# One written order for all five engines from attention into the experts, and the last batch's routing moved in among the early tiles

## The chip, the cores and the metric

The kernel runs on one core of a Trainium2 chip. That core has TensorE (PE in the profile; its weight loads stand apart as PEld), VectorE (DVE), ScalarE (ACT), GpSimd (POOL) and SyncE (SP). Each engine works through its own queue of instructions in that queue's order, and engines wait for each other through semaphores. The metric is the device time of one execution in microseconds (us), the median of several runs. The profile is one further execution, and its span is the time from the first to the last instruction of the core.

## What is computed

Two blocks follow each other. The first is an attention in which a query sees only the keys of its own hash bucket (six sign bits of a random projection). The second sends each token to one of eight experts.

```python
B, H, S, D = 4, 8, 768, 64
mask   = bucket(q)[:, :, :, None] == bucket(k)[:, :, None, :]
scores = where(mask, q @ k.T / sqrt(D), -1e9)
attn   = exp(scores - max);  attn = attn / (sum(attn) + 1e-9)
x      = (attn @ v) as (B*S, H*D)                       # 3072 tokens, 512 wide
logits = (x/|x|) @ (emb/|emb|).T / tau                  # 8 experts
e      = argmax(logits);  gate = softmax(logits)[e]
out    = gate * (relu(x @ w1[e]) @ w2[e])               # w1: 512 x 1024, w2: 1024 x 512
```

## The kernel before

**Attention.** The 32 heads are taken as 16 pairs (`pairs`, four pairs for each of four batches). A pair has 12 units: two halves of the queries by six chunks of 128 keys. For one unit `scores` does the matmuls (L541, L544), an exponential on ACT (L547) and a running sum over the chunks on DVE (L551, L554); `attend` multiplies by the values (L566). The main loop (L676) takes three units at a time, g = 0 to 3 within a pair, and hangs one piece of side work on each g: loads and transposes for pairs to come, `sums` and `scale` for the softmax denominators of the pair before, `store` of finished rows to DRAM (`xd`), and the routing of the batch before (`logits`, `turn_logits`, `route`, `gates`, `begin`/`place`, `fill`, `lists`, `places`). The last pair has no successor to hang its denominators on; `scale_last` does them after the loop.

**Experts.** Tokens of one expert lie in tiles of 128. `fetch` gathers the rows of a tile from `xd` by four indirect DMAs on POOL (L376) into one of four buffers `xgs`, and the tile's gates by one more (L384). `turn` transposes the gathered rows on DVE (L395). `hidden` is the first layer: for each of eight blocks f, TensorE fills one of four PSUM banks `ps_h` (L906) and ACT evicts it through a relu into `ht` (L908). `result` is the second layer (L914), the weighting by the gate on DVE (L918) and a scatter to the output by an indirect DMA on POOL (L919). Each expert has `KT` = 3 planned tiles. For the experts 0 and 1 (`EARLY` = 2) the first two tiles hold tokens of the first three batches alone, so they run before the last batch is routed. Their third tiles (`late`), and all tiles of the experts 2 to 7, need the last batch's places. Tokens beyond the planned tiles come at the end in up to `NO` further tiles behind run-time conditions.

**What sets the order.** A planner orders each engine's instructions from its own estimate of costs. `in_order(begun)` (L416) overrules it: it chains all instructions of an engine since `begun` in the order in which the program is written. It is called once, at L753, at the end of attention. What is written behind that call, the expert stage, is ordered by the planner, which may also place such an instruction between two of attention's. Three `tc.issue_after` blocks (L1000, L1033, L1046/L1051) tie single pieces of routing behind one instruction.

The stretch that the change touches most is this one, between attention and expert 2:

```python
hidden(0, early[0][0], 2 * P)                                     # L989
early[1:] = [turn(got) for got in early[1:]]
lt = logits(b, ssq[b], ps_x(), sp)
result(0, early[0][1][0:1]);  l = turn_logits(...);  route(b, l, sp);  result(0, early[0][1][1:])
count(...);  place(...);  gates(...)
hidden(1, ..., range(0, 6));  fill(...);  hidden(1, ..., range(6, NF));  places(lists(...), ...)   # L1003-L1006
late = [tiles_of(e, 2) for e in range(EARLY)]
result(1, ...);  late = [turn(got) for got in late];  result(1, ...)
for e in range(EARLY):  hidden(e, late[e][0], P);  ...;  result(e, late[e][1])
```

Of the kernel before, what the change touches and what calls it, by code (L numbers as in the profile page):

```python
# [16 lines left out]
P = 128  # L17
# [9 lines left out]
def kernel(  # L27
# [341 lines left out]

    def fetch(src, pos, t, n, width=N + 1):  # L370
        parts = []
        for i in range(n):
            xg = xgs[taken[2] % len(xgs)]
            taken[2] += 1
            for g in range(NQ):
                nc.gpsimd.indirect_dma_start(  # L376
                    out=xg[:, g, :], out_offset=None, in_=xd[0 : width * NQ, :],
                    in_offset=bass.IndirectOffsetOnAxis(ap=pos[:, t + i, g : g + 1], axis=0))
            parts.append(xg)
        tiles = []  # L380
        for i in range(n):
            g = ggs[taken[1] % len(ggs)]
            taken[1] += 1
            nc.gpsimd.indirect_dma_start(out=g[:], out_offset=None, in_=gd[:, :],  # L384
                                         in_offset=bass.IndirectOffsetOnAxis(ap=src[:, t + i : t + i + 1], axis=0))
            tiles.append((i, g, src[:, t + i : t + i + 1]))
        return parts, tiles


    def turn(got):  # L390
        parts, tiles = got
        x = xgt[taken[0] % EARLY if taken[0] < 2 * EARLY else EARLY + taken[0] % NX]
        taken[0] += 1
        for i, xg in enumerate(parts):
            nc.vector.transpose(x[:, :, i * P : (i + 1) * P].rearrange("p c (g t) -> p g c t", t=32),  # L395
                                xg[:].rearrange("p g (c f) -> p g c f", f=32))
        return x, tiles

# [25 lines left out]
    with ExitStack() as at:  # L424
# [52 lines left out]
        def load(pr):  # L477
# [5 lines left out]
            for g in range(NQ):  # L483
                for i, src in enumerate((q, k)):
                    (nc.scalar if pr == 0 and i else nc.sync).dma_start(
                        qk[32 * g : 32 * (g + 1), i].rearrange("t (c a) f -> t c a f", c=NC),
                        src[b, 2 * j + g // 2].rearrange("(a t c) d -> t c a d", t=32, c=NC)[
                            :, :, :, 32 * (g % 2) : 32 * (g % 2 + 1)])
            nc.sync.dma_start(vt[:], v[b, 2 * j : 2 * j + 2].rearrange("h (p c) d -> p h c d", c=NC))
            ld[pr] = (qk, vt)  # L490


# [122 lines left out]

        def scale_last(pr):
            b, j = pairs[pr]
            z = op.tile([P, 2, SH], F32, name="zl", tag="acc", bufs=3)
            ps = banks()
            for s in range(2):  # L620
                for h in range(2):
                    nc.tensor.matmul(ps[h * D : (h + 1) * D, s, 0:SH], lhsT=ones[:, 0:D], rhs=acc[pr, s][:, h, :],
                                     start=True, stop=True)
            for s in range(2):
                nc.scalar.activation(z[:, s], ps[:, s, 0:SH], ACT.Copy, bias=TINY * S)
            t = rp.tile([P, S], F32, name="xx", tag="junk", bufs=2)
            for s in range(2):
                nc.vector.reciprocal(out=z[:, s], in_=z[:, s])
                x = xs(b)[:, j, s * SH : (s + 1) * SH]
                nc.vector.tensor_tensor(out=x, in0=x, in1=z[:, s], op=ALU.mult)  # L630
                nc.vector.tensor_tensor(out=z[:, s], in0=x, in1=x, op=ALU.mult)
            x = xs(b)[:, j - 1]
            nc.vector.tensor_tensor(out=t[:], in0=x, in1=x, op=ALU.mult)
            nc.vector.tensor_tensor(out=t[:], in0=t[:], in1=z[:].rearrange("p s n -> p (s n)"), op=ALU.add)
            nc.vector.tensor_tensor(out=ssq[b][:], in0=ssq[b][:], in1=t[:], op=ALU.add)
# [31 lines left out]
        for pr in range(3):  # L667
            load(pr)
            if pr == 0:
                nc.sync.dma_start(emb[:], expert_emb[:, :])  # L670
                nc.sync.dma_start(tau_t[:], tau.unsqueeze(0).broadcast_to([E, 1]))
        for i in range(2):
# [3 lines left out]
        for u0 in range(0, U + G, G):  # L676
# [7 lines left out]
            for u in range(u0, u0 + G):  # L684
                if u < U:
                    scores(u)
            if end and j == 2 and g == 3:
                places(listed, pos[0][:], NS, banks()[:, 0], rp)
                early = [fetch(src[0], pos[0], 0, 2, ZC + 1)]
            for u in range(u0 - G, u0):  # L690
                if 0 <= u < U:
                    attend(u)
            if pr == len(pairs):
                break
# [12 lines left out]
            elif g == 1:  # L707
                prep_features(pr + 1, 1)
                if pr > 0:
                    scale(pr - 1)  # L710
                load(pr + 3)
                if NP <= pr < NP + 2 * ND:
                    piece(pr - NP)
# [7 lines left out]
                if j == 3 and end:  # L721
                    for e in range(1, EARLY):
                        early.append(fetch(src[0], pos[0], e * KT, 2, ZC + 1))
                    bound(0)
# [13 lines left out]
            else:  # L738
# [9 lines left out]
                if j == 3 and end:  # L748
                    early[0] = turn(early[0])
        store(len(pairs) - 2)  # L750
        scale_last(len(pairs) - 1)
        store(len(pairs) - 1)
        in_order(begun)  # L753

# [122 lines left out]
    with ExitStack() as mo:  # L877
# [21 lines left out]
        ys = [mp.tile([P, DM], F32, name=f"y{i}") for i in range(3)]  # L899
        made, done, turned = [0], [None], [None]  # L900

        def hidden(i, xt, n, fs=range(NF)):
            for f in fs:
# [4 lines left out]
                nc.scalar.activation(ht[:, f, 0:n], ph[:, 0:n], ACT.Relu)  # L908

        def result(i, tiles):  # L910
            for j, gate, src in tiles:
                py = ps_y()
                for f in range(NF):
                    done[0] = nc.tensor.matmul(py[:], lhsT=ht[:, f, j * P : (j + 1) * P], rhs=w2s[i][:, f, :],  # L914
                                               start=(f == 0), stop=(f == NF - 1)).ins
                y = ys[made[0] % len(ys)]
                made[0] += 1
                turned[0] = nc.vector.tensor_scalar_mul(y[:], py[:], gate[:, 0:1]).ins  # L918
                nc.gpsimd.indirect_dma_start(out=out[:, :], out_offset=bass.IndirectOffsetOnAxis(ap=src, axis=0),  # L919
                                             in_=y[:], in_offset=None, bounds_check=N - 1, oob_is_err=False)  # L920

        def tiles_of(e, first):
            return fetch(src[1], pos[1][:], e * KT + first, KT - first)

# [63 lines left out]
        b = B - 1  # L988
        hidden(0, early[0][0], 2 * P)  # L989
        early[1:] = [turn(got) for got in early[1:]]  # L990
        lt = logits(b, ssq[b], ps_x(), sp)
        result(0, early[0][1][0:1])
        l = turn_logits(lt, ps_x(), sp)
        route(b, l, sp)
        result(0, early[0][1][1:])
        ps = ps_x()
        count(b, ps[:, 0 : E * NC], ps[:, E * NC : 2 * E * NC])
        for ins in place(b, ps[:, 0 : 2 * E * NC].rearrange("p (t n) -> p t n", t=2), sp):
            pass
        with tc.issue_after(ins.ins):  # L1000
            for i in range(3):
                gates(b, sp, i)
        hidden(1, early[1][0], 2 * P, range(0, 6))  # L1003
        fill(b, ps_x()[:, 0 : 4 * NS])
        hidden(1, early[1][0], 2 * P, range(6, NF))
        places(lists(slots, src[1][:], NS, sp), pos[1][:], NS, ps_x(), sp)  # L1006
        late = [tiles_of(e, 2) for e in range(EARLY)]
        result(1, early[1][1][0:1])
        late = [turn(got) for got in late]
        result(1, early[1][1][1:])  # L1010
        for e in range(EARLY):
            hidden(e, late[e][0], P)
            if e == 0:
                nxt = turn(tiles_of(EARLY, 0))
            bring1(e, EARLY + e)
            result(e, late[e][1])
            bring2(e, EARLY + e)
# [6 lines left out]
        for e in range(EARLY, E):  # L1024
            i = e % NW
            x, tiles = nxt
            if e + 1 < E:
                nxt = turn(tiles_of(e + 1, 0))
            else:
                nxt = turn(fetch(osrc, opos[:], 0, 1))  # L1030
            hidden(i, x, KT * P)
            if e == EARLY:
                with tc.issue_after(turned[0]):  # L1033
                    ctl, ocol = beyond_tiles()
            if e + NW < E:
# [9 lines left out]
            if e == EARLY + 1:  # L1045
                with tc.issue_after(done[0]):  # L1046
                    oslots = beyond_fill(ocol)
            elif e == EARLY + 2:
                osrc = sp.tile([P, NO], U32, name="osrc")
                opos = sp.tile([P, NO, NQ], U32, name="opos")  # L1050
                with tc.issue_after(done[0]):  # L1051
                    places(lists(oslots, osrc[:], NO, sp), opos[:], NO, ps_x(), sp)
        nt = nc.values_load(ctl[0:1, 2 * NO : 2 * NO + 1], min_val=0, max_val=NO)
        with ExitStack() as rest:  # L1054
            for t in range(NO):
# [3 lines left out]
                if t + 1 < NO:  # L1059
                    nxt = turn(fetch(osrc, opos[:], t + 1, 1))  # L1060
                hidden(i, x, P)
# [40 lines left out]
```

## Time and profile before

| what | number |
|---|---|
| time, median of 3 runs (lowest, highest) | 828.38 us (827.16, 828.94) |
| span of the profiled execution | 826.0 us |
| PE busy | 723.6 us, 88% |
| DVE / ACT / POOL busy | 357.7 / 268.2 / 221.7 us |
| mean granted TensorE clock | 0.940 |

The span falls into stages: a start without TensorE of some 10 us, attention up to about 375 us, a hand-over up to about 388 us, the experts from there. The busy share of TensorE in 40 slices is the first thing to read, since TensorE is the fullest engine; the second is the row of the clock that was granted to it. A slice is 20.65 us long. "Idle before" in a group or a timeline is the time that the engine stood still just before the instruction, followed by what ended it.

### The profile page before, as it was taken

Reading aid. Unit: us, or ns where it says so; the run is one execution under the profiler, and the core shown is the slowest. Engines: PE = TensorE matmul, PEld = TensorE weight load, DVE = VectorE, ACT = ScalarE, POOL = GpSimd, SP = SyncE. Lnnn points to the kernel's source line nnn. Section 1 sums busy time; section 2 is a strip of 40 time slices with the busy share of each in tenths; the row PEclk is TensorE's granted clock in tenths of the full one; section 3 lists DMA queues with packets and bytes.
Section 4 is the critical chain, followed back from the end, with each engine's and each line's share of the span. In section 5 each row is a group of like instructions: output and inputs, shape, how many; then the busy total and the mean of one; then the engine's idle time right before and its main releaser. Section 6 shows DMA issues by size and latency. Waiting matters only on the chain.

```text
span 826.0 us, 10015 instructions
## 1 busy us (share of the span) xinstructions
PE 723.6 (88%) x3669; PEld 360.4 (44%) x3669; DVE 357.7 (43%) x664; ACT 268.2 (32%) x432; POOL 221.7 (27%) x222
## 2 busy tenths in 40 slices
PE   4999999989998999794998113999999999999993
PEld 2444444434443444342675002654545454545481
DVE  4777887887789787855241100031100101010000
ACT  2776666656664656450110000110101010101010
POOL 4011121011211111164027772107170521010051
PEclk9999999999999999896999555999999999999997
DMA  9546546646656752223601211834343433333340
GB/s 140 91 79 97 90 85 129 118 82 115 120 106 113 123 98 39 40 56 72 206 26 42 67 48 42 302 114 164 115 165 108 153 125 128 114 128 114 128 141 20
DMA packets 198171, 87.56 MB, mean 106 GB/s; under 512 B 171473, under 2 KB 179469, under 8 KB 198104
## 3 DMA queue, kind: packets, MB, share of 16 engines
q1 hardware_dynamic: 188408, 72.94, 37.2%
q0 software_dynamic: 6560, 13.41, 4.9%
q10 hardware_dynamic: 3136, 0.39, 0.4%
q8 instruction: 33, 0.54, 0.3%
q14 instruction: 34, 0.28, 0.1%
HBM read 82.31 MB, written 13.31 MB: 116 GB/s over the span
## 4 chain that ended last, share of the span: by engine, by line
PE 39%; another core or an unknown queue 6%; issue 5%; POOL 1%; ACT 0%; POOLq 0%; ACTq 0%
PE ps_h L906 20%; PE ps_y L914 18%; POOL xg L376 1%; POOL out_dram L919 0%; ACT ht L908 0%; PE ps_x L192 0%; POOL gg L384 0%; PE ps_x L981 0%; PE ps_x L200 0%; PE ps_x L322 0%; ACTq L908 0%; PE ps_x L337 0%; POOLq L1054 0%; POOLq L919 0%
## 5 line engine op out<-in xcount | busy, mean ns | idle before, releaser
L914 PE MATMUL ps_y<-w,ht 128*128 128x512 f32 x416 | 182.1, 596 | 0.0
L547 ACT ACTIVATE p<-banks 128x768 f32<-128x768 f32 x192 | 154.2, 812 | 78.4 <-PE banks L544 76.3
L541 PE MATMUL banks<-qt,kt 64*128 64x384 f32 x768 | 166.1, 510 | 8.4 <-DVE z L586 6.5
L908 ACT ACTIVATE ht<-ps_h 128x384 f32<-128x384 f32 (+2 forms) x96 | 38.2, 402 | 369.4 <-PE ps_h L906 257.1
L554 DVE TENSOR_TENSOR acc<-acc,p 128x768 f32<-128x768 f32 x128 | 139.7, 1092 | 13.4 <-issue 1.7
L566 PE MATMUL av<-p,vt 128*64 128x385 f32 x768 | 142.4, 508 | 0.0
L906 PE MATMUL ps_h<-xgt,w 128*128 128x384 f32 (+1 forms) x512 | 139.6, 434 | 0.0
L914 PEld LDWEIGHTS ps_y<-w,ht 128*128 128x128 f32 x416 | 79.0, 191 | 96.0 <-issue 94.2
L376 POOL DMA_INDIRECT xg<-xd,pos x96 | 93.4, 973 | 84.4 <-DVE xgt L395 52.1
L906 PEld LDWEIGHTS ps_h<-xgt,w 128*128 128x128 f32 x512 | 87.4, 190 | 52.2 <-issue 2.9
L918 DVE TENSOR_SCALAR y<-ps_y,gg 128x512 f32<-128x512 f32 x26 | 19.4, 747 | 205.2 <-PE ps_y L914 181.5
L541 PEld LDWEIGHTS banks<-qt,kt 64*128 64x128 f32 x768 | 65.7, 189 | 74.0 <-issue 39.8
L906 PE MATMUL ps_h<-xge,w 128*128 128x256 f32 (+1 forms) x256 | 50.3, 361 | 54.0 <-issue 48.8
L603 POOL TENSOR_TENSOR xT<-xT,rz 128x768 f32<-128x768 f32 x15 | 29.4, 1961 | 235.4 <-DMA rz<-zd 235.4
L566 PEld LDWEIGHTS av<-p,vt 128*64 128x64 f32 x768 | 50.6, 139 | 78.5 <-issue 75.1
L919 POOL DMA_INDIRECT out_dram<-y,src x24 | 24.3, 1012 | 181.4 <-DVE y L918 126.7
L395 DVE STREAM_TRANSPOSE xgt<-xg 128x512 f32<-128x512 f32 x21 | 14.0, 695 | 134.2 <-PE ps_h L906 88.0
L906 PEld LDWEIGHTS ps_h<-xge,w 128*128 128x128 f32 x256 | 44.1, 215 | 61.2 <-issue 50.5
L544 PE MATMUL banks<-qb,kb 64*128 64x384 bf16 x384 | 64.4, 325 | 0.3 <-DVE kb L530 0.3
L551 DVE TENSOR_TENSOR acc<-p,p 128x768 f32<-128x768 f32 x32 | 30.6, 958 | 27.2 <-ACT p L547 27.1
L544 PEld LDWEIGHTS <-kb 64*128 64x128 bf16 x384 | 19.9, 95 | 26.5 <-DVE kb L530 1.7
L410 POOL TENSOR_TENSOR ssq__163<-ssq__163,xsq 128x768 f32<-128x768 f32 x10 | 18.8, 1876 | 43.7 <-ACT xsq L408 43.7
(241 smaller groups left out, 389.5 us busy)
## 6 DMA issues: line engine op xcount, KB each, us to landing
w<-in_moe_w_dram SPq DMA_DIRECT2D x22, 2048.0 KB
qk<-in_q_dram SPq DMA_DIRECT2D x64, 96.0 KB
vt<-in_v_dram SPq DMA_DIRECT2D x16, 384.0 KB
xd<-xb SPq DMA_DIRECT2D x64, 96.0 KB
qk<-in_k_dram SPq DMA_DIRECT2D x60, 96.0 KB
rz<-zd SPq DMA_DIRECT2D x30, 192.0 KB
w<-in_moe_w_dram SPq DMA_DIRECT2D x8, 512.0 KB
xg<-xd,pos POOLq DMA_INDIRECT x96
```

Source lines behind the costliest of these rows:

```text
L376: nc.gpsimd.indirect_dma_start(out=xg[:, g, :], out_offset=None, in_=xd[0 : width * NQ, :], in_offset=bass.IndirectOffsetOnAxis(ap=pos[:, ...
L541: nc.tensor.matmul(ps[:, h, 0:SH], lhsT=kt[rows[h], c // HC, kc], rhs=qt[rows[h], s, :], start=True, stop=False)
L544: nc.tensor.matmul(ps[:, h, 0:SH], lhsT=kb[rows[h], c // HC, kc], rhs=qb[rows[h], s, :], start=False, stop=True)
L547: nc.scalar.activation(p[:, :, 0:SH], ps[:, :, 0:SH], ACT.Exp, scale=ESCALE)
L551: nc.vector.tensor_tensor(out=a[:], in0=pts[(u - 1) % NPT][:, :, 0:SH], in1=p[:, :, 0:SH], op=ALU.add)
L554: nc.vector.tensor_tensor(out=a[:], in0=a[:], in1=p[:, :, 0:SH], op=ALU.add)
L566: nc.tensor.matmul(ps[h * D : (h + 1) * D, 0 : SH + 1], lhsT=vt[:, h, c, :], rhs=p[:, h, 0 : SH + 1], start=(c == 0), stop=(c == NC - 1))
L603: nc.gpsimd.tensor_tensor(out=x, in0=x, in1=rz[:].rearrange("p s n -> p (s n)"), op=ALU.mult)
L906: nc.tensor.matmul(ph[:, 0:n], lhsT=w1s[i][:, d, f * P : (f + 1) * P], rhs=xt[:, d, 0:n], start=(d == 0), stop=(d == ND - 1))
L908: nc.scalar.activation(ht[:, f, 0:n], ph[:, 0:n], ACT.Relu)
L914: done[0] = nc.tensor.matmul(py[:], lhsT=ht[:, f, j * P : (j + 1) * P], rhs=w2s[i][:, f, :], start=(f == 0), stop=(f == NF - 1)).ins
L919: nc.gpsimd.indirect_dma_start(out=out[:, :], out_offset=bass.IndirectOffsetOnAxis(ap=src, axis=0), in_=y[:], in_offset=None, bounds_check ...
```

## The change

All engines follow one written order through the expert stage too. `in_order(begun)` is no longer called at the end of attention but in the expert loop, at e = E - NW = 6, behind that expert's `hidden`; the `tc.issue_after` blocks go. Since the program's order now decides, the program is rewritten:

- `fetch` is split into `fetch` (rows) and `gated` (gates), `turn` takes the rows alone, and `result` is split into `second` (matmuls), `weigh` (DVE) and `send` (scatter).
- The last pair's denominators are done in halves: `scale_last(pr, s)` and `scaled_last(pr, s)`, the first half within the loop's last step, the second behind it; the squares of the pair before go to ACT (`squares_before`).
- The last batch's logits, routing and slots are written in between the blocks f of the early tiles, and the gathers of the late tiles and of expert 2 follow at once.
- In the loop over the experts, the gathers and transposes of the next expert are written ahead of the `hidden` of the present one.
- The places of the first three batches' tiles and the first early gathers come behind the three `attend` of their step, not ahead of them.
- At the start the k loads of pair 1 go to the ACT queue as pair 0's do, and the loads of the values come behind the next pair's q and k.

```diff
-            if end and j == 2 and g == 3:
-                places(listed, pos[0][:], NS, banks()[:, 0], rp)
-                early = [fetch(src[0], pos[0], 0, 2, ZC + 1)]
             for u in range(u0 - G, u0):
                 if 0 <= u < U:
                     attend(u)
+            if end and j == 2 and g == 3:
+                places(listed, pos[0][:], NS, banks()[:, 0], rp)
+                early = [fetch(pos[0], 0, 2, ZC + 1)]
...
                 if j == 3 and end:
-                    early[0] = turn(early[0])
-        store(len(pairs) - 2)
-        scale_last(len(pairs) - 1)
+                    scale_last(pr, 0)
+                    squares_before(pr - 1, rp)
+                    early_x = [turn(early[0])]
+                    early_g = [gated(src[0], e * KT, 2) for e in range(EARLY)]
+                    scaled_last(pr, 0)
+                    store(pr - 1)
+        scale_last(len(pairs) - 1, 1)
+        scaled_last(len(pairs) - 1, 1)
+        nc.vector.tensor_tensor(out=ssq[B - 1][:], in0=ssq[B - 1][:],
+                                in1=zcs[len(pairs) - 1][:].rearrange("p s n -> p (s n)"), op=ALU.add)
         store(len(pairs) - 1)
-        in_order(begun)
...
         b = B - 1
-        hidden(0, early[0][0], 2 * P)
-        early[1:] = [turn(got) for got in early[1:]]
+        hidden(0, early_x[0], 2 * P, range(0, NF // 2))
         lt = logits(b, ssq[b], ps_x(), sp)
-        result(0, early[0][1][0:1])
+        early_x.append(turn(early[1]))
+        hidden(0, early_x[0], 2 * P, range(NF // 2, NF - 2))
         l = turn_logits(lt, ps_x(), sp)
+        hidden(0, early_x[0], 2 * P, range(NF - 2, NF))
         route(b, l, sp)
-        result(0, early[0][1][1:])
+        result(0, early_g[0][0:1])
         ps = ps_x()
         count(b, ps[:, 0 : E * NC], ps[:, E * NC : 2 * E * NC])
         for ins in place(b, ps[:, 0 : 2 * E * NC].rearrange("p (t n) -> p t n", t=2), sp):
             pass
-        with tc.issue_after(ins.ins):
-            for i in range(3):
-                gates(b, sp, i)
-        hidden(1, early[1][0], 2 * P, range(0, 6))
+        last_ = second(0, 1)
+        hidden(1, early_x[1], 2 * P, range(0, 1))
         fill(b, ps_x()[:, 0 : 4 * NS])
-        hidden(1, early[1][0], 2 * P, range(6, NF))
-        places(lists(slots, src[1][:], NS, sp), pos[1][:], NS, ps_x(), sp)
-        late = [tiles_of(e, 2) for e in range(EARLY)]
-        result(1, early[1][1][0:1])
-        late = [turn(got) for got in late]
-        result(1, early[1][1][1:])
+        half_ = lists(slots, src[1][:], NS, sp)
+        hidden(1, early_x[1], 2 * P, range(1, 2))
+        places(half_, pos[1][:], NS, ps_x(), sp)
+        send(weigh(last_, early_g[0][1][1]), early_g[0][1][2])
+        gates(b, sp, 0)
+        gates(b, sp, 1)
+        hidden(1, early_x[1], 2 * P, range(2, NF))
+        late = [fetch(pos[1][:], e * KT + 2, 1) for e in range(EARLY)]
+        late_x = [turn(late[0])]
+        gates(b, sp, 2)
+        late_x.append(turn(late[1]))
+        nxt = fetch(pos[1][:], EARLY * KT, KT)
+        late_g = [gated(src[1], e * KT + 2, 1) for e in range(EARLY)]
+        result(1, early_g[1])
+        nxt = turn(nxt), gated(src[1], EARLY * KT, KT)
...
             if e + 1 < E:
-                nxt = turn(tiles_of(e + 1, 0))
+                nxt = turn(fetch(pos[1][:], (e + 1) * KT, KT)), gated(src[1], (e + 1) * KT, KT)
...
             hidden(i, x, KT * P)
             if e == EARLY:
-                with tc.issue_after(turned[0]):
-                    ctl, ocol = beyond_tiles()
+                ctl, ocol = beyond_tiles()
+            if e == E - NW:
+                in_order(begun)
```

## The prediction

> **What bounds the kernel now.** I read the slices of the page first. TensorE is full in attention (slices 2 to 17) and again from slice 26; in between it stands nearly still, at half clock, while POOL is fullest.
>
> ```profile
> PE   4999999989998999794998113999999999999993
> POOL 4011121011211111164027772107170521010051
> PEclk9999999999999999896999555999999999999997
> ```
>
> The busy time by stage sizes this:
>
> ```profile
> 374.00:388.00 14.00, 3.10 (x13) 0.87 (x10) 5.87 (x8) 1.61 (x4) 7.98 (x9) 0.69 0.12 33
> 448.00:512.00 64.00, 10.99 (x61) 9.68 (x60) 6.24 (x9) 1.62 (x7) 41.54 (x44) 0.55 0.16 49
> 536.00:786.00 250.00, 250.00 (x716) 130.25 (x715) 30.46 (x63) 23.85 (x49) 66.76 (x69) 1.00 0.37 129
> ```
>
> (Columns: PE, PEld, DVE, ACT and POOL busy, granted clock, DMA share, GB/s.) From 536 us TensorE leaves nothing to gain by order. So the change lives in two holes, and in a small one within attention.
>
> The large hole. The chain of waits goes through ACT's evictions of the late tiles' first layer, and cannot name what released them:
>
> ```profile
> 461.58 21.37 another core or an unknown queue
> ...
> 483.32 21.34 another core or an unknown queue
> ...
> 505.01 5.96 another core or an unknown queue
> ```
>
> The timeline of ACT shows the same gaps:
>
> ```profile
> 461.30 0.28 ACT L908 ACTIVATE ht<-ps_h 128x128 f32<-128x128 f32 x1 [26.17 <-issue]
> 483.04 0.28 ACT L908 ACTIVATE ht<-ps_h 128x128 f32<-128x128 f32 x1 [21.46 <-remote]
> 504.73 0.28 ACT L908 ACTIVATE ht<-ps_h 128x128 f32<-128x128 f32 x1 [21.42 <-remote]
> 511.05 0.79 ACT L908 ACTIVATE ht<-ps_h 128x128 f32<-128x128 f32 x4 [6.04 <-remote]
> ```
>
> The matmuls of these four banks are recorded as done by 452.14. The semaphore that ACT waits for is TensorE's own; its updates show in the trace at 482.95, 504.65 and 510.97, and then three more within 0.3 us. The signals were held; TensorE, with all four `ps_h` full, waited for ACT. During this POOL issues 56 indirect DMAs in one unbroken run (432.22 to 502.65), because the planner lets it gather for the experts 2, 3 and 4 at once. Smaller delays of the same semaphore stand behind other runs: 2.4 us at 362.37 (a run of 10), 1.6 and 2.0 us at 576.8 and 579.4 (18), 1.3 and 2.2 us at 618 and 619 (16). After 7 to 11 gathers in a row it came on time at 441.72, 569.97 and 611.21. I read this as: a long run of indirect DMAs holds up TensorE's signals; why, no view says.
>
> The small hole, in the timeline around the end of attention:
>
> ```profile
> 378.30 0.71 DVE L395 STREAM_TRANSPOSE xge<-xg 128x512 f32<-128x512 f32 x1 [6.33 <-DMA xg<-xd,pos]
> 378.93 0.92 DVE L554 TENSOR_TENSOR acc<-acc,p 128x768 f32<-128x768 f32 x1
> 383.58 0.71 DVE L395 STREAM_TRANSPOSE xge<-xg 128x512 f32<-128x512 f32 x1 [3.73 <-DMA xg<-xd,pos]
> 384.22 0.92 DVE L554 TENSOR_TENSOR acc<-acc,p 128x768 f32<-128x768 f32 x1
> 385.19 1.55 PE L622 MATMUL banks<-acc,ones 128*64 128x384 f32 x4 [9.93 <-DVE acc L554]
> ```
>
> The planner put the transposes of expert 1's tiles ahead of attention's last two sums on DVE. They wait for gathers that POOL only starts at 371.30, and the denominators wait behind them. Third, in pair 14:
>
> ```profile
> 345.92 0.32 PE L337 MATMUL banks<-half__3125,pick 128*128 128x48 bf16 x4 [3.71 <-DVE half__3125 L329]
> 346.17 4.12 PE L566 MATMUL av<-p,vt 128*64 128x385 f32 x12
> ```
>
> **What the Trainium skill says.** "TensorE: Matmul & The Clock Gate", Part 1, has the array fall to half clock after an idle window of some 3.4 us and come back after as long a busy one. The trace agrees: the clock is 0.5 from 345.17 to 352.0, 379.3 to 393.0 and 454.4 to 515.8, and the twelve matmuls above take 4.12 us where others take 2.16. "Perfetto Trace Analysis", Tensor Engine Instruction, says that a matmul's end is estimated and that its update follows the acknowledged write, so 452.14 is no proof that the banks were full. The same page, Sequencer Loop, has each engine instruction wait in its queue for its semaphores; what DVE did above agrees. "DMA: Bandwidth & Descriptors", Anatomy of one DMA, gives some 2 us of fixed cost; the trace has the first early gather issued at 349.96 and landed at 352.4.
>
> **The change part by part.** Before's PE times are followed to where expert 2 starts, 535.4 us.
>
> *Attention.* With `places` behind the three `attend` (2.16 us at full clock), 1.5 us of the 3.71 us wait is left, since DVE's half_ stays at 345.88: 2.2 us. A gap so short has not dropped the clock elsewhere (1.22 us at 368.29), so the 6.1 us at half clock become 3.1: 3.0 us. Sum 5.2. The loads moved at the start I cost at nothing: 6144 small packets at some 1000 per us for pair 1, then the values, are in by 17 to 18 us, and the first `attend` is at 21.0.
>
> *Hand-over.* In written order DVE finishes attention's sums by 373.9, so all eight denominator matmuls (0.8 us) run with or right behind the last `attend`, at 375.7. ACT copies, and `hidden` starts at 376.9, not 387.70: 10.8 us. No 10 us gap means no half clock in 387.7 to 393.0: 2.6 us. What is added: DVE now runs, one after another, squares 1.0, transposes 1.4, the first half's reciprocal and two products 3.7, a store's transpose 1.0, the second half 3.7 and the sum 1.0, from 374.5 to 386.3; the logits behind four blocks of `hidden` (6.9 us) come to TensorE at 383.8 plus 1.25 of their own that need neither. They wait some 1.3 to 2.5 us; I take 2.5. Squares on ACT (0.83) and the halving hide behind it. Net 10.9 us.
>
> *Routing among the early tiles.* TensorE's work is unchanged. `count` is followed by `second` (7.0 us) and one block (1.7); DVE's weighting and `place` took 0.75 + 5.7 us (420.42 to 426.75), so `fill` doesn't wait. `lists` (0.7) hides behind the next block. `weigh(last_)` and the gates stand ahead of ACT's next evictions by about 2 us, within the four banks. Nothing.
>
> *Late tiles.* Places are ready at about 413. POOL then issues one scatter, 8 late gathers, 12 of expert 2 and 2 of gates: 23 at 1.26 us, to 442. Then it must stop for scatters that need TensorE's results; that is the cure: it can't run 56 in a row. TensorE goes on through `hidden(1)` (to 422), `result(1)` (to 436), the late tiles (7.2 + 7.0 twice) to 464.7. Late rows are turned by 426, ten us early; weights of expert 1 are asked for at 390, and two 2 MB loads took 6 to 8 us each, so they are in by 407. Removed: the gaps 9.49, 19.65, 19.62 and 4.24 = 53.0, and half clock behind them: four groups of 8 matmuls at 2.08 instead of 0.93 (4.6), 2.6 us of `result` (1.3). Sum 58.9. But 23 in a row is beyond the 10 to 18 behind which delays were seen. If held from the 13th on (430), the late blocks fill four banks by 440 and wait until POOL stops and the signals come, 446: 6 us left. The bounds are 0 and, held from the sixth on so that even `hidden(1)`'s last blocks are caught, 19.
>
> *Expert loop.* POOL now does three scatters, 12 row and 3 gate gathers per expert in a fixed order, 22.7 us of the 41.2 that TensorE needs, and turns end about 24 us in. DVE and SP have slack as before. The gathers now run during `hidden` instead of `result`. At expert 4 `places` comes behind the last weighting and `lists` on DVE: 1.2 us of waiting for TensorE, new.
>
> Sum: 5.2 + 10.9 + 58.9 - 6 - 1.2 = 67.8. 828.4 - 67.8 = 760.6, say 760.
>
> **Rivals.** *No hold at all:* the 6 us go too, 754. For it: no run longer than 23, the 11 gathers of 557 to 570 harmed nothing. Against: 18 and 16 did delay signals.
>
> *The hold comes back in each expert.* Now 15 gathers fall on the `hidden` phase, where TensorE needs ACT every 2.6 us and has four banks of slack. Held from the tenth gather on, only the last blocks are late and `result` needs them later still: nothing. Held from the fourth on (at 802 to 808 five gathers and a scatter were enough to hold two signals), block 6 waits from 15.5 to 23.9 us: 8.4 us for each of five experts, 42 us: 754 + 42 = 796. Against: at 787 to 792 five gathers in a `hidden` phase delayed nothing.
>
> *Slower.* If signals are held through whole runs of 16 (20.1 us), and `hidden` waits for each in experts 2 to 6, 100 us come on top of 754: 854. Only the big hole speaks for it, and there the runs were over three times as long. DVE's transposes ahead of the weightings could also lock in, but they end 3 us before the first weighting.
>
> **How the numbers follow.** Forecast 0.46, no hold 0.26, hold in each expert 0.20, slower 0.06; 0.02 for a gain that is lost exactly. The range, 750 to 797, takes in the first three, with 4 us below 754 for a logits wait that doesn't come. Faster 0.92, same 0.02, slower 0.06.
>
> **What would show it.** Right: DVE's L554 ahead of all L395 of expert 1, `hidden` starting near 377 (370 to 372 if pair 14's gain comes first), ACT's L908 without gaps of 20 us, expert 2 starting near 465 minus these 5, PE full up to the end. Wrong: ACT gaps put down to an unknown queue within `hidden` of experts 2 to 6; a DVE chain so long that the logits wait over 5 us; weights of expert 1 landing late because both loads now queue behind both stores.

## The result, and the profile after

The changed kernel takes 775.62 us (median of 4 runs, 772.76 to 777.73) against 828.48 us before (827.16 to 828.94): 0.936 of the time, 95% interval 0.933 to 0.940. 760 was forecast, with 750 to 797 as range. The slices of the page, to be laid beside those of before:

```profile
PE   4999999989999899988899879999999989999993
POOL 4010022120211111106613722617171543520150
PEclk9999999998999899999999979999999999999997
```

Before had three slices at half clock (23 to 25), with TensorE nearly idle in them; one dent is left (slices 23 and 24), and POOL's block of 77 has become a pattern that repeats with each expert. The hand-over, on TensorE's timeline:

```profile
376.44 2.11 PE L573 MATMUL av<-p,vt 128*64 128x385 f32 x12
378.38 0.82 PE L630 MATMUL banks<-acc,ones 128*64 128x384 f32 x4
380.31 1.97 PE L927 MATMUL ps_h<-xge,w 128*128 128x256 f32 x8 [1.11 <-ACT zl L632]
```

The 9.93 us that the denominators waited for DVE are gone; `hidden` starts 1.1 us after the last denominator matmuls. What is left of the holes, on ACT's timeline at the late tiles and at expert 5:

```profile
452.46 0.72 ACT L929 ACTIVATE ht<-ps_h 128x128 f32<-128x128 f32 x3 [24.74 <-remote]
...
634.29 0.87 ACT L929 ACTIVATE ht<-ps_h 128x384 f32<-128x384 f32 x2 [6.54 <-remote]
```

In both, signals of TensorE reach ACT late ("held" from here on), as in the hole of before. TensorE stands still for 7.3 us between 442.87 and 452.24, and for 2.8 us at 632, with half clock from 446.5 to 456.8 and from 634.3 to 637.7.

The first of the two differs from the hole of before in one point, and TensorE's timeline shows it:

```profile
440.81 2.06 PE L927 MATMUL ps_h<-xge,w 128*128 128x128 f32 x17
443.82 0.27 PE L927 MATMUL ps_h<-xge,w 128*128 128x128 f32 x1 [0.95 <-issue]
445.23 0.27 PE L927 MATMUL ps_h<-xge,w 128*128 128x128 f32 x1 [1.13 <-issue]
447.33 0.37 PE L927 MATMUL ps_h<-xge,w 128*128 128x128 f32 x1 [1.83 <-issue]
...
452.24 5.98 PE L927 MATMUL ps_h<-xge,w 128*128 128x128 f32 x32 [0.34 <-issue]
```

A block is eight matmuls. In before TensorE ran through four blocks at full speed, until all four banks were full, and then waited for ACT. Here it stops one matmul into the third block, with one of the four banks not yet begun, goes on by single matmuls, and runs again at 452.24, ahead of ACT's first eviction at 452.46. So it does not wait for a bank. Its signals due from 440.98 to 442.76 come at 452.29 to 452.48. A stop of the same kind, 0.9 us in the middle of a block, ends at 392.13, when a signal due at 387.45 comes at 392.16. Why TensorE itself stops in these two places is not shown; the other traces have no such stop inside a block of `hidden` that lasts over 0.6 us.

POOL's runs of indirect DMAs beside the two gaps count 24 (418.39 to 448.41) and 20 (606.04 to 630.95). The other experts have runs of 16, and there TensorE waits for nothing, although signals are held there too: at expert 2 those due from 490.42 to 498.16 come at 497.36 and 503.8. In these runs some held signals came through while the run went on; the last ones came 3.5 to 5.1 us after the start of the run's last DMA.

Attention ends later than before, not earlier. From TensorE's timeline there:

```profile
79.49 0.92 PE L548 MATMUL banks<-qt,kt 64*128 64x384 f32 x4 [2.01 <-DVE enT L477]
...
355.38 0.92 PE L548 MATMUL banks<-qt,kt 64*128 64x384 f32 x4 [1.82 <-DVE pos L342]
```

Neither wait was there before. Both are `scores` that wait for a PSUM slot which something else of the `banks` still holds: the transposes of the experts' embeddings (copied by DVE to `enT`) in the first case, the places in the second.

### The profile page after: what moved, and what is told of

It reads as the page before. It is cut to its first block, busy times and chain, and to the rows that moved or that the text cites. A ratio compares the mean times of both kernels' runs of the same rounds, so it can differ in the third digit from the quotient of the medians.

```text
span 776.0 us, 9999 instructions
## 1 busy us (share of the span) xinstructions
PE 721.9 (93%) x3669; PEld 358.5 (46%) x3669; DVE 359.0 (46%) x663; ACT 268.1 (35%) x433; POOL 221.6 (29%) x222
## 3 DMA queue, kind: packets, MB, share of 16 engines
q0 software_dynamic: 6560, 13.41, 5.4%
## 4 chain that ended last, share of the span: by engine, by line
PE 73%; DVE 8%; issue 6%; DMA 5%; POOL 4%; ACT 1%; another core or an unknown queue 1%; SPq 1%; DVEq 0%; POOLq 0%; ACTq 0%
PE ps_h L927 21%; PE ps_y L935 21%; PE banks L548 13%; PE av L573 13%; PE banks L551 3%; DVE acc L561 2%; POOL xg L376 2%; PE banks L526 2%; DMA rz<-zd 1%; PE banks L590 1%; DMA xd<-xb 1%; DMA zd<-zc 1%; DVE xb L616 1%; DMA proj<-in_proj_dram 1%
## 5 line engine op out<-in xcount | busy, mean ns | idle before, releaser
L927 PE MATMUL ps_h<-xge,w 128*128 128x256 f32 (+1 forms) x256 | 47.5, 342 | 9.4 <-issue 8.3
L927 PEld LDWEIGHTS ps_h<-xge,w 128*128 128x128 f32 x256 | 41.5, 204 | 15.8 <-issue 10.9
```

Source lines behind the costliest of these rows:

```text
L927: nc.tensor.matmul(ph[:, 0:n], lhsT=w1s[i][:, d, f * P : (f + 1) * P], rhs=xt[:, d, 0:n], start=(d == 0), stop=(d == ND - 1))
```

## The experiments

The kernel before does not take the same time on every chip. The runs fell on four chips, called A to D here; runs of one chip are compared with that chip's own runs of the kernel before. All runs of a chip were taken together, so that "chip" stands for the chip or for what else differed at that time.

| chip | before, us (runs) | what ran there |
|---|---|---|
| A | 829.05 (23) | first to fourth |
| B | 767.83 (11) | fifth to eighth |
| C | 768.69 (27) | ninth to eleventh |
| D | 830.54 (11) | twelfth |

The times on record (828.5 and 775.6) are of the kind of A and D.

### POOL alone in written order (chip A)

```diff
+            if alone is not None and ins.engine != alone:   # in in_order
+                continue
...
         in_order(begun)
+        done_at = len(nc.cur_bb.bb.instructions)
...
             hidden(i, x, KT * P)
+            if e == E - NW:
+                in_order(done_at, mybir.EngineType.Pool)
```

> The kernel before, with one thing changed: POOL's instructions of the expert stage follow the written order up to expert 6, the other engines stay with the planner. POOL then can't issue 56 indirect DMAs in one run; the longest is about 20. Theory (a long unbroken run of indirect DMAs holds up TensorE's signals): the hole of 59 us between 452 and 511 shrinks to under 15 us, time 770 to 785; the hole at the hand-over (10 us before the denominators) stays or shrinks with it. Rival (the planner's order on TensorE, ACT or DVE makes the hole, POOL only fills it): the hole stays within 10 us of what it was, time 815 or more.

Measured: 786.07 us, 0.949 (0.945 to 0.953). The 9.92 us ahead of the denominators stay; of the large hole one gap is left:

```profile
473.93 2.08 PE L909 MATMUL ps_h<-xge,w 128*128 128x128 f32 x8 [6.61 <-issue]
```

TensorE's and ACT's instructions come in the same order in this trace and in before's, and 43 us are gone. So the large hole came with POOL's run. The hand-over's gap has another origin: DVE's order there is the one of before, with expert 1's transposes ahead of the last sums.

### The lock alone, on the text of before (chip A)

```diff
         store(len(pairs) - 1)
-        in_order(begun)
...
             hidden(i, x, KT * P)
+            if e == E - NW:
+                in_order(begun)
```

> The kernel before, with its own text, but the written order of all engines reaches to expert 6 instead of the end of attention. It has none of the rewriting (no halves, gathers with their gates, routing written behind the early tiles). Theory: both holes are the planner's, so the lock alone brings most of the gain: hand-over hole gone (10 us), large hole under 15 us, time 770 to 785. Rival (the rewriting is what makes the order good; the old text in written order makes new waits at the routing of the last batch and at the late tiles): 790 to 830, with gaps of over 5 us on TensorE between 400 and 480.

Measured: 771.18 us, 0.930 (0.927 to 0.933). This is the whole gain of the change; it is 0.6% below the changed kernel's 775.62, with the intervals just touching. The hand-over's gap is gone, and gaps of 3.8 us at 361, 7.3 at 458 and 2.8 at 628 to 632, beside held signals, remain.

### The new text, ordered by the planner (chip A)

```diff
         store(len(pairs) - 1)
+        in_order(begun)
...
-            if e == E - NW:
-                in_order(begun)
```

> The changed kernel's text, but the written order ends with attention as before, and the planner orders the experts. Theory: the planner again lets POOL run far ahead, a run of over 40 indirect DMAs comes back, and with it a hole of 40 to 60 us; time 810 to 830. Rival (the rewriting alone removes the holes): under 790.

Measured: 829.11 us, 0.999 (0.997 to 1.001). Both holes are back, here from ACT's timeline:

```profile
493.21 0.28 ACT L930 ACTIVATE ht<-ps_h 128x128 f32<-128x128 f32 x1 [21.41 <-remote]
512.81 0.28 ACT L930 ACTIVATE ht<-ps_h 128x128 f32<-128x128 f32 x1 [19.32 <-remote]
```

and the denominators wait 9.98 us again. Halving the last sums and moving the routing among the early tiles bring nothing by themselves; behind the lock the planner decides, and POOL's run has 56 DMAs again.

### A quarter of the bytes in each gather (chip A)

```diff
+    for t in xgs:
+        nc.gpsimd.memset(t[:], 0.0)
...
-                    out=xg[:, g, :], out_offset=None, in_=xd[0 : width * NQ, :],
+                    out=xg[:, g, 0:32], out_offset=None,
+                    in_=xd[0 : width * NQ, :].rearrange("n (a f) -> (n a) f", f=32),
```

> The kernel before, but each row gather moves 32 of a row's 128 numbers (the rest of the gathered rows stays zero and the wrong rows are read, so the experts compute on other data; the routing is untouched). Number and order of the indirect DMAs are the same, their bytes a quarter. If the number of indirect DMAs in a run is what holds TensorE's signals, the hole stays at 50 to 65 us, 815 to 830. If it is the bytes that the DMA engines write into SBUF, it falls to under 25 us, under 795.

Measured: 829.94 us (one run), with ACT's gaps of 22.15 and 20.03 us. The software queue moved 8.10 MB instead of 13.41. So it isn't the bytes. The number of DMAs in the run is unchanged, and so is the queue's number of packets (6560); between these two the run can't tell.

### The gathers twice (chip B)

```diff
                     in_offset=bass.IndirectOffsetOnAxis(ap=pos[:, t + i, g : g + 1], axis=0))
+                if twice:                                 # experts 3 to 7
+                    nc.gpsimd.indirect_dma_start(
+                        out=spill[g][:], out_offset=None, in_=xd[0 : width * NQ, :],
+                        in_offset=bass.IndirectOffsetOnAxis(ap=pos[:, t + i, g : g + 1], axis=0))
```

> The changed kernel, with each row gather of the experts 3 to 7 issued twice, the second time into a scratch tile that nobody reads. POOL then has 24 + 3 gathers in a row beside each hidden phase, 34 us, and with the three scatters 37.8 us of work per expert, still under TensorE's 41.2. Theory (a long run of indirect DMAs holds TensorE's signals until about 4 us after its last one starts): blocks of the hidden phase wait for the end of the run, 10 to 18 us more per expert for five experts, with half clock behind: 830 to 880 us. Rival (only POOL's own work counts, and it still fits): 775 to 785 us and no ACT gaps over 3 us in the hidden phases.

Measured: 786.48 us, 1.024 (1.022 to 1.026) of before on this chip. The theory fails here: in a run of 28 DMAs (467.7 to 502.9) every signal of TensorE comes within 0.02 us of its matmul. TensorE loses its time elsewhere:

```profile
509.14 3.78 PE L940 MATMUL ps_y<-w,ht 128*128 128x512 f32 x4 [8.13 <-DVE y L947]
```

On DVE the weightings are written behind the next expert's transposes. Those now wait for the last gathers (the third one starts at 499.81), and `beyond_tiles` runs behind them at expert 2 until the weightings start at 508.34. `ps_y` has two banks, so the third tile's matmuls wait: 8.1, 6.9 and 9.1 us at the experts 2, 4 and 6. The rival was wrong too: POOL's work fits in sum, but what waits for its end does not.

### Pauses on POOL, and the last gathers tied (chip B)

```diff
             parts.append(xg)
+            if pause:                                     # late tiles, experts 2 to 7
+                nc.gpsimd.memset(pad[:], 0.0)             # 128x1536, took 1.40 us
```

> The changed kernel, with a memset of 128x1536 numbers on POOL (an estimated 2.4 us, from 0.27 us for 128x160) behind each tile's four row gathers of the late tiles and of the experts 2 to 7: no run of indirect DMAs is longer than four, and POOL does more work in all. Theory: the signals come through in the pauses, so the seven gaps of 7.3 us at the late tiles and the 2.8 us at expert 5 go, with the half clock behind them: 762 to 768 us. Rival (it is the number of DMAs in a stretch, or a POOL that is busy with anything): the holds stay or grow, 776 to 790 us.

```diff
+                with tc.issue_after(sent[0].ins):         # the last scatter of expert 6
+                    nxt = fetch(opos[:], 0, 1)
-                nxt = turn(fetch(opos[:], 0, 1)), gated(osrc, 0, 1)
+                nxt = turn(nxt), gated(osrc, 0, 1)
```

> The changed kernel, with the four gathers of the first tile beyond the plan tied behind expert 6's last scatter, so that they no longer stretch the run beside expert 5's hidden phase from 16 to 20. Theory: the 2.8 us gap at 632 and the 1.6 us of half clock behind it go, the rest stays: 771 us, 0.994 of the changed kernel. Rival (the hold at expert 5 has another cause): 775 to 776 us, gap unchanged.

Measured: 759.44 us with pauses, 0.989 (0.988 to 0.991), and 757.01 us tied, 0.987 (0.984 to 0.989). Neither trace has a gap at the late tiles or at expert 5. The changed kernel itself wasn't run on chip B; on chip C it took 0.988 of before, and both are the same as that. There was nothing to cure, so these two runs decide nothing.

### The gathers spread (chip B)

```diff
-                nxt = turn(fetch(pos[1][:], (e + 1) * KT, KT)), gated(src[1], (e + 1) * KT, KT)
+                nx = turn(fetch(pos[1][:], (e + 1) * KT, 1))
...
-            result(i, tiles)
+                result(i, tiles[0:1])
+                a = fetch(pos[1][:], (e + 1) * KT + 1, 1)
+                result(i, tiles[1:2])
+                turn(a, nx, 1)
+                a = fetch(pos[1][:], (e + 1) * KT + 2, 1)
...
+                turn(a, nx, 2)
```

> The changed kernel, with the gathers spread by the written order instead of pauses: one tile's four gathers ahead of an expert's hidden phase and one behind each of its first two scatters, likewise for expert 2 among the late tiles; the last tile beyond the plan tied as in the run before; the lock reaches to expert 6's results. No run of indirect DMAs is longer than 12. Theory: no signal is late enough to stop TensorE from 440 us on, so the 7.3 us at the late tiles with some 2 us of half clock and the 4.4 us at expert 5 go: 762 us. Rival (gathers in the result phase delay the weightings behind the transposes on DVE, or hold signals there): 766 to 776 us, with gaps ahead of the result matmuls.

Measured: 789.67 us, 1.027 (1.024 to 1.030) of before. That is a loss, as the rival said, but in another place: the rival looked for gaps ahead of the second layer's matmuls, and they stand ahead of the next expert's first layer.

```profile
707.33 2.29 PE L928 MATMUL ps_h<-xgt,w 128*128 128x384 f32 x3 [7.34 <-DVE xgt L399]
```

The last four gathers (696.28 to 700.07) come behind the second scatter, and their rows are in, and transposed, only at 706.57, when TensorE has nothing else to do. Such waits for rows are 2.0 to 7.5 us, ahead of the experts 3, 4, 6 and 7.

### Before and after on a chip without the hole (chip C)

The ninth run is the kernel before unchanged, the tenth the changed kernel unchanged, the eleventh the pauses again.

> The kernel before, unchanged, for its trace beside the changed kernel on one chip. On the chip of the runs with gathers twice, pauses, tied and spread, it took 767.8 us against 829 on the chip of the first four runs. Theory (the hold of TensorE's signals behind a long run of indirect DMAs is a matter of the chip or of the session): where it takes 768, its trace has no gaps of 20 us on ACT although POOL still issues some 56 indirect DMAs in a row, and keeps the 9.9 us ahead of the denominators. Where it takes 829, the gaps are there again. Rival (the planner's order or POOL's run came out different): no run of 56.

> The changed kernel, unchanged, beside the kernel before on the same chip. Theory: if before takes 768 here, only what has nothing to do with held signals is left of the gain: the hand-over's 10.9 us and attention's 1 to 5, less the 0.9 us at expert 4: 757 us, 0.985. If before takes 829 here: 775 us, 0.936 as on record. Rival (the lock is worth its 53 us on every chip): 715 us where before takes 768.

> The changed kernel with the memsets on POOL behind each tile's gathers once more, beside the changed kernel itself. If before takes 829 here (signals are held), theory: pauses let the signals through, 763 to 768 us against 775 of the changed kernel; rival: 776 to 790. If before takes 768 here (no signals held): the pauses have nothing to cure, 757 to 760, the same as the changed kernel within 0.3%.

Measured, in this order: 769.28 us, 1.000 (0.999 to 1.002) of chip C's other runs of before; 758.96 us, 0.988 (0.985 to 0.991); 760.36 us, 0.988 (0.984 to 0.992). The slices of the kernel before on this chip:

```profile
PE   4999999989999899969499998999999999999993
POOL 4010111120110212106601477756624402020150
PEclk9999999999999999998779999999999999999997
```

POOL issues 58 indirect DMAs in one run from 432.25 to 505.92, two more than in the profile of before. TensorE stays full beside them, and ACT evicts the late tiles' blocks one after the other:

```profile
449.58 0.28 ACT L908 ACTIVATE ht<-ps_h 128x128 f32<-128x128 f32 x1 [14.43 <-PE ps_h L906]
450.47 0.28 ACT L908 ACTIVATE ht<-ps_h 128x128 f32<-128x128 f32 x1 [0.62 <-PE ps_h L906]
```

So the order is worth 53 us on one chip and 10 us on another, with the same program. What is left on C is mainly the hand-over: 10.87 us ahead of the denominators and the half clock behind it in before, 1.4 us ahead of `hidden` in after.

### The lock alone, with longer pauses (chip D)

```diff
             parts.append(xg)
+            for _ in range(2 * pause):                    # on the text of the lock alone
+                nc.gpsimd.memset(pad[:], 0.0)
```

> The text of the kernel before with the lock's call moved behind expert 6's first layer (as in the run of the lock alone), and two memsets of 1.4 us each on POOL behind each tile's four row gathers from the late tiles on. The lock alone took 771.2 us where before takes 829, with 3.8 + 7.3 + 2.8 us of gaps by held signals and some 6 us of half clock behind them. If before takes 768 here (no held signals): those 20 us are gone, 751 to 756 us, which is 3 to 8 under the changed kernel's 759; rival (the rewritten text is worth something once no signal is held): 759 to 765. If before takes 829 here: the two later gaps go if pauses let signals through, 757 to 762; rival (the number of DMAs counts, not the pauses): 770 to 778.

Measured: 769.84 us, 0.927 (0.924 to 0.930), which is far from the theory's 757 to 762 and just outside the rival's 770 to 778. The trace answers the question all the same. Expert 4's last evictions on ACT's timeline, first in the run of the lock alone (chip A), then here:

```profile
583.47 1.26 ACT L907 ACTIVATE ht<-ps_h 128x384 f32<-128x384 f32 x3 [6.52 <-remote]
```

```profile
577.78 0.49 ACT L910 ACTIVATE ht<-ps_h 128x384 f32<-128x384 f32 x1 [2.09 <-PE ps_h L908]
580.36 0.49 ACT L910 ACTIVATE ht<-ps_h 128x384 f32<-128x384 f32 x1 [2.09 <-issue]
```

The `hidden` phases of the experts 2 to 5 now have their evictions 2.6 us apart to the end, and the gaps of 7.3 and 2.8 us are gone; the latest eviction at the late tiles came 0.9 us after its matmuls. That chip D does hold signals is seen in the same trace where POOL's runs are not cut, behind the early gathers (a run of 10, 377.40 to 390.45) and near the end (a run of 6, 740.95 to 748.26):

```profile
390.91 0.38 ACT L910 ACTIVATE ht<-ps_h 128x256 f32<-128x256 f32 x1 [5.33 <-PE ps_h L908]
...
749.70 0.45 ACT L910 ACTIVATE ht<-ps_h 128x128 f32<-128x128 f32 x2 [3.32 <-remote]
```

The first of these evictions comes 4.4 us after its matmuls, the second 3.6. So with the run cut into fours and fives by 2.83 us of other work, the hold is gone on a chip that has it elsewhere. The gain was given back at once:

```profile
472.76 3.57 PE L908 MATMUL ps_h<-xgt,w 128*128 128x384 f32 x5 [8.09 <-DVE xgt L398]
```

The five pauses up to expert 2's last tile are 14 us of POOL's time, its rows are turned at 472.00, and half clock lasts to 478.5.

## Why the prediction was right, step by step

The time lies in the range, 15.6 us above the number. Compared by TensorE's milestones, the forecast put the span's end at 826.0 - 67.8 = 758.2; it came at 776.0. The 17.8 us divide so:

| step | forecast | measured | off |
|---|---|---|---|
| last `attend` starts | 5.2 earlier | 3.9 later (374.13 to 378.06) | 9.1 |
| from there to `hidden` | 13.6 - 10.8 = 2.8 | 2.25 | -0.5 |
| `hidden` to expert 2 | 147.7 - 2.6 + 2.5 - 52.9 = 94.7 | 99.6 | 4.9 |
| expert 2 to the last result | 277.0 + 1.2 = 278.2 | 282.5 | 4.3 |

*Attention: the step that failed.* Its own term was right: `places` behind the `attend`s left a wait of 1.52 us (1.5 forecast), without half clock, and TensorE gained 5.3 us there (5.2 forecast): it ran 5.65 us behind before's times ahead of that spot and 0.36 behind it. What failed is that all else in attention was put at nothing: the loads in so many words, the slots and the half clock by silence. Most of the 9.1 us is found in these places:

- The wait for `enT`, 2.0 us. It is in every trace of the new text (also in the third run, which has the planner's experts) and in none of the old one. Late loads are not its cause: the embeddings are first used at 53.5 us (52.5 before), and DVE copies `enT` 3.9 us after the transposes in both kernels (74.22 to 78.12 before, 75.26 to 79.25 after). In before the third `scores` of that step start at 76.54, ahead of the copy; now they wait for it, so they have been given another slot. Why the slots fall differently is not shown.
- The places hold a slot that the next `scores` want: 1.8 us, just behind the wait that was shortened.
- The half clock behind the two 2.9 us waits for `z` (the denominators' sums) lasted 6.8 us each time instead of 3.4: some 2.5 us. Before's trace had shown that waits shorter than 3.4 us can be followed by half clock (2.92 us at 171.09 and at 261.85, each with 3.4 us behind it), which the forecast passed over when it took 3.4 us of idleness as what drops the clock.
- At 369, 0.6 us of waits for ACT, whose signals from TensorE are held behind a run of 8 gathers (355.52 to 366.75).
- 0.6 us is no loss: the first half's denominators now stand ahead of the last three `attend`s.
- The first `attend` came 1.0 us later; over all traces it varied from 19.75 to 22.06 us, so this says nothing of the change.

On chip C attention ends 1.1 us later than before.

*Hand-over.* As forecast, to 0.5 us: both `scale_last` run beside the last `attend`s. The wait for the logits was 0.5 + 0.3 us on record, not 2.5, beside the 0.9 us stop in the middle of a block named above; on chip C, which has no such stop, it was 0.5 + 1.7. The lock does this, not the halving: the lock alone has the same 1 us between the last denominators and `hidden`.

*Routing among the early tiles.* It cost nothing, as forecast, and nothing shows that it brought anything: the run of the lock alone doesn't have it and gains as much.

*Late tiles.* DVE's transposes ahead of the weightings did not lock in here, but the run with gathers twice shows how near that was. The removal of the large hole and a hold beside the run of 23 (it was 24) came as argued. The forecast without a hold for the stretch from `hidden` to expert 2, 94.7 - 6 = 88.7 us, is what the changed kernel shows on chip C: 88.73. With it, 99.6 were measured, so the hold cost 10.9 us instead of 6: the gaps were 7.3, and I had not charged the half clock behind them. Its path was another one than forecast, too: not four full banks, but TensorE stopped in the third. That the estimate of 6 us comes near is in part luck.

*Expert loop.* On chip C the loop is 1.1 us longer than before; 1.2 was forecast. On the chip on record it is 5.5. The rival "the hold comes back in each expert" was right in that signals are held in the experts 2 to 6, and wrong in the cost: the forecast's case of four banks of slack held where the run is 16, and TensorE had no gap there. At expert 5 the planner hoisted four more gathers (the tiles beyond the plan, written behind the lock) into the run; that made 20, and 2.8 us and half clock followed. That the four are the cause was not settled: the tied run fell on a chip that holds no signals.

*The mechanism.* "A long run of indirect DMAs holds up TensorE's signals" is shown for chips A and D: cutting the run by order (first run) takes away the gaps of 20 us and leaves one of 6.6, pauses in it (last run) take away the hold, and a quarter of the bytes doesn't. A pause breaks the run and also makes DMAs fewer per time; which of the two counts is not separated. It is no rule for all chips: on B and C runs of 28 and 58 held nothing. The gain of 52.9 us therefore hangs on a chip that holds signals (the same edit gained 9.7 us on C), and the forecast, drawn from one such trace, had no means to see that. What differs between the chips stays open: no trace shows it, no run switches a chip from one kind to the other, and since all runs of a chip were taken together, the time at which they ran is not ruled out.

*The better version.* Lock alone at 0.930 is the fastest on chips that hold signals except for its variant with pauses (0.927), whose interval overlaps it. On the chips without the hold nothing beat the changed kernel beyond the intervals, and the lock alone wasn't run there.

## What to carry to other kernels

When an engine waits for a signal that another engine has long been due to give, look at what runs on a third engine at that time, and, if that is a long run of indirect DMAs, break it by order before touching the two that wait; but price a pause like any other work on that queue. Where a wait is moved out of a spot, ask at once which buffer the moved work now holds, and for whom. And take the time of the kernel before on more than one chip before a gain is called a property of the program: here the same edit was worth 6% on one and 1% on another.

## What the hardware showed that I had not expected

- The same program took 828 to 831 us on some chips and 768 to 769 us on others, with nearly the same traces up to the first long run of indirect DMAs.
- Where signals are held, several come together. In the changed kernel's runs of 16 to 24 the last came 3.5 to 5.1 us after the start of the run's last DMA, in before's run of 56 they came 9.3 us after it (510.97), and during that run one came through every 21.7 us.
- While its signals were held, TensorE stopped in the middle of a block, with a bank to spare, for 7.3 us in all (442.87 to 452.24). In before it had run through four blocks at full speed while five signals were held.
- The changed kernel's 2.0 us wait for `enT` was followed by 3.4 us of half clock on chip C and by none in the profile on record; its 2.9 us wait for `z` ending at 174 was followed by 6.8 us on record and by 3.4 on chip C, and the second one, at 266, by 6.8 us on record and by none on C.
